# Four-layer sliding/full attention: pieces of four in one layer only, two key projections a chunk later, two weight slices in exponential buffers

## The chip, the cores and the metric

The kernel runs on one core of one Trainium2 chip. The metric is the device time of one execution in microseconds (us). TensorE does the matrix products, ScalarE (ACT) the exponentials, VectorE (DVE) and GpSimd (POOL) the elementwise work, and SyncE (SP) issues all DMAs in one order. "The clock" is TensorE's granted clock as a share of full speed.

## The reference

Four layers on x of shape [1, 2048, 512], 32 heads of 16. Layers 0 and 2 use weights A and a causal window of 256 tokens; layers 1 and 3 use weights B and attend to all tokens. Each layer adds its attention to x.

```python
def _A_ref(x, wqkv, wo):          # _B_ref is the same without the mask
    qkv = (x @ wqkv).reshape(B, S, 3, H, Dh).transpose(2, 0, 3, 1, 4)
    q, k, v = qkv[0], qkv[1], qkv[2]
    scores = jnp.einsum("bhqd,bhkd->bhqk", q, k) * (Dh ** -0.5)
    mask = (idx[:, None] - idx[None, :] >= 0) & (idx[:, None] - idx[None, :] < W)   # W = 256
    p = _softmax(jnp.where(mask[None, None], scores, -1e9), axis=-1)
    o = jnp.einsum("bhqk,bhkd->bhqd", p, v)
    return o.transpose(0, 2, 1, 3).reshape(B, S, D) @ wo

x = A_x
x = x + _A_ref(_layernorm(x), A_wqkv, A_wo)
x = x + _B_ref(_layernorm(x), B_wqkv, B_wo)
x = x + _A_ref(_layernorm(x), A_wqkv, A_wo)
x = x + _B_ref(_layernorm(x), B_wqkv, B_wo)
```

## The kernel before

**Attention.** The 2048 tokens are cut into four chunks of 512 queries. `attention(l, works)` goes through the chunks, and in each through eight groups of four heads (quads). A quad takes three steps in a sliding layer (24 steps a chunk) and sixteen in a full one. A step issues scores (line 722, TensorE) and two exponentials (line 726, ScalarE) into buffers with the tag `e`, of which there are six. In a sliding layer GpSimd then masks the edges of the window in place (lines 789 and 792). The product with the values (line 799 sliding, line 766 full) is issued two steps later. After that comes a share of *side work*.

**Side work.** All projections (queries, keys, values, output), the normalisations and the transposes of the neighbouring chunks and of the next layer are written as generators, wrapped in `Work` objects, and issued between the steps. Their matmuls have line 437, twelve to a group in one accumulation bank. The names are used below: `K(l, c)`, `Q(l, c)` and `VV(l, c)` are the keys, queries and values of chunk c of layer l, 48 matmuls each where all is done at once; `K3(c, ht)` and `Q3(c, ht)` are a quarter of those for layer 3 (12 matmuls, one group of 128 features `ht`); `OO(l, c)` is the output projection with the residual, after which the chunk's normalisation follows; `T(l, c)` transposes the normalised chunk by DMA (SyncE, line 497) into the `xc` tiles that the projections of layer l read; `NN` and `PR` are layer 0's normalisations and the preparation of weights; `F` fills buffers.

**Which side work belongs to which chunk** is written by hand: `side0(c)` and `side2(c)` for the chunks of layers 0 and 2, `tails[l]` and `lasts[l]` for what follows a sliding layer's last chunk. Whatever of a chunk's list is left over at its end is forced out there (`sd.finish()`), waiting where it has to.

**The planner.** TensorE's order is fixed as written. A small clock in the program adds 0.222 us for each matmul, and a `Work` is taken only when its dependencies are due by that clock. In each step of a sliding chunk, side work is issued up to the part of the list's cost that is due. `PH["run"]` says how many matmuls of a group are issued at once. It is set for each chunk: four if the list's cost is below seven matmuls a step, twelve otherwise. That gives four in chunk 0 of layer 0 and in all chunks of layer 2, and twelve in chunks 1 to 3 of layer 0.

```python
                if win:
                    PH["run"] = RUN if sd.cost < FEW * MM * sd.steps else 12
```

The order on the other engines and on SyncE's queue is worked out by the framework's scheduler from the program's order and priorities. SyncE's queue runs in order: an issue that waits for its source or its destination keeps back all behind it.

**Weights.** `weights(ty, s, n, ...)` loads a projection's weights from the DRAM tile `wd` into one of two buffers with the tag `w` (lines 398 and 400). A quarter of a projection takes a slice of 128 columns, 256 KB. A `Work` marked to use weights is opened, its load issued, only if the user of the buffer two places back is done; the planner then waits 8 us before its first matmul. `all_of(works, following)` issues a list of work to its end and may open the weights of the first of the following works.

**The tail of layer 2** is the list `tails[2]`, behind its last chunk, and then `lasts[2]`: K3(2,0), the output projection of the last chunk with its normalisation, four parts of the values, Q3(0,0), T(3,3) and K3(3,0), until layer 3's first scores can start.

Of the kernel before, what the change touches and what calls it, by code (L numbers as in the profile page):

```python
# [9 lines left out]
F32 = mybir.dt.float32  # L10
BF16 = mybir.dt.bfloat16
F16 = mybir.dt.float16
# [7 lines left out]
P = 128  # L20
NT = S // P
NC = D // P
HT = P // DH
NHT = H // HT
QC = 512
# [6 lines left out]
MM = 0.222  # L32
HEAD_START = 100
EB, XB, XNB, WB, VB, OB = 6, 4, 4, 2, 3, 5
RUN, FEW = 4, 7
L_MIN = 2.0 ** -90
L_SUM = 2.0 ** 60

# [149 lines left out]
def fast_path(ctx, tc, flag, a_x, a_wqkv, a_wo, b_wqkv, b_wo, out):  # L188
# [29 lines left out]
    def wait(us):  # L218

        return "wait", clock[0] + us  # L220
# [170 lines left out]

    def weights(ty, s, n, f0=0, f1=D):

        if (ty, s) in WT:
            return WT.pop((ty, s))
        w = wp.tile([P, NC, 2, D], F16, name=f"w{n}", tag="w", bufs=WB)
        if f1 - f0 == D:
            nc.sync.dma_start(w, wd[ty, s])
        else:
            nc.sync.dma_start(w[:, :, :, :f1 - f0], wd[ty, s][:, :, :, f0:f1])  # L400
        return w
# [103 lines left out]
    def project(l, s, c, act, ht=None, first=None):  # L505


        ty, n = l % 2, f"{l}_{s}_{c}" + ("" if ht is None else f"_h{ht}")
        if not first:
            w = weights(ty, s, n, *((0, D) if ht is None else (ht * P, (ht + 1) * P)))  # L510
            yield wait(8)
            xc = XC[l, c]
        if s == 0:
            dst = rows(qs[ty, c])
        elif ty == 0:
            dst = rows(kw[c])
        else:
            dst = rows(kf)[:, :, c * QC:(c + 1) * QC]
        sqs = {}
        for t in range(NHT) if ht is None else (ht,):  # L520
            ps = bank()
            w0 = t * P if ht is None else 0
            if first:
                yield from mms(ps, [(first[0][:, k, t * P:(t + 1) * P], first[1][:, k, :]) for k in range(NC)])
            else:
                yield from mms(ps, [(w[:, k, a, w0:w0 + P], xc[:, b, k, :]) for k in range(NC) for a, b in TERMS], 2.2)
            settle(not sqs)
            sp = vp.tile([P, 2, QC], F16, name=f"sp{n}_{t}", tag="sp", bufs=3)
            e = first[2][:, t:t + 1] if first else es[:, ty, s, t:t + 1]
            with tc.high_priority(HEAD_START):  # L530
                if act:
                    nc.scalar.activation(sp[:, 0], ps, AF.Copy, scale=e)  # L532
                else:
                    nc.vector.tensor_scalar(sp[:, 0], ps, e, None, op0=ALU.mult)  # L534
                nc.vector.scalar_tensor_tensor(sp[:, 1], ps, e, sp[:, 0], op0=ALU.mult, op1=ALU.subtract)  # L535
            sq = vp.tile([P, QC], BF16, name=f"sq{n}_{t}", tag="sq", bufs=NHT)
            if act:
                nc.scalar.activation(sq, sp[:, 0], AF.Square)
            else:
                nc.gpsimd.tensor_tensor(sq, sp[:, 0], sp[:, 0], ALU.mult)  # L540
            sqs[t] = sq

            d = dst[8 * t:8 * t + 8].rearrange("h (d b) n -> (h d) b n", b=4)
            if s:
                nc.sync.dma_start(d[:, 0:2], sp[:, 0:1].broadcast_to([P, 2, QC]))
                nc.sync.dma_start(d[:, 2], sp[:, 1])
            else:
                nc.sync.dma_start(d[:, 0:2], sp)
                nc.sync.dma_start(d[:, 2], sp[:, 0])
            yield -MM if PH["full"] else -PH["run"] * MM  # L550
        return sqs
# [409 lines left out]
    def later(f, *a):  # L961

        yield from f(*a)
# [4 lines left out]
    def attention(l, works):  # L968

        win = l % 2 == 0  # L970
        phase(l)
        load = load_win if win else load_full
        sd = None
        for t in range(NHT if l == 3 else 1):
            for c in range(NQ):
                qds = range(2 * t, 2 * t + 2) if l == 3 else range(NQD)
                if l == 1:

                    sd = sd or Side(NT * NQD // 2, works[0], works[1], 0.33)
                    while ("Q", 1, c) not in DONE:  # L980
                        sd.one(True)
                    settle()
                else:
                    sd = Side((3 if win else NT) * len(qds), works[t * NQ + c], works[t * NQ + c + 1], 0.34 if l == 3 and t < 2 else 0.0)
                if win:
                    PH["run"] = RUN if sd.cost < FEW * MM * sd.steps else 12
                ops = load(l, c, qds[0])
                for qd in qds:
                    if (l, c, qd) == (1, 0, NQD // 2):
                        sd.finish()  # L990
                        sd = Side(NT * NQD * NQ - NT * NQD // 2, works[1], works[2], 0.33)
                    nxt = load(l, c, qd + 1) if qd + 1 in qds else None
                    a = acc[qd % 2 if win else 0]
                    began = clock[0]
                    for f in (attn_win if win else attn_full)(l, c, qd, *ops, a):
                        clock[0] = max(clock[0], began + (2.4 if win else 1.8))
                        began = clock[0]
                        pvq.append([f])
                        flush(2)
                        sd.step()  # L1000
                        if win and not (PH["unit"] and PH["extra"]):
                            settle(False, 1 if PH["unit"] else 9)
                    pvq[-1].append(lambda l=l, c=c, qd=qd, a=a: epilogue(l, c, qd, a))
                    ops = nxt
                if l != 1 or c == NQ - 1:
                    sd.finish()
                if not win:
                    settle()
        flush(0)
        phase(None)  # L1010

    def T(l, c):
        return Work(later(lambda: transpose(l, c, XN.pop((l, c), ()))), 0.0, ("T", l, c), [("N", l, c)], aside=True)

    def K(l, c, act=True):
        return Work(later(keys, l, c, act), PK, ("K", l, c), [("T", l, c), ("P", l % 2, 1), ("P", l % 2, 0)], True)

    def Q(l, c, act=True, after=()):
        k = [("K", l, i) for i in (c - 1, c) if i >= 0] if l % 2 == 0 else list(after)
        return Work(later(queries, l, c, act), PK, ("Q", l, c), [("T", l, c), ("P", l % 2, 0)] + k, True)  # L1020

    def K3(c, ht, act=False):
        return Work(later(keys, 3, c, act, ht), PK / 4, ("K3", c, ht), [("T", 3, c)], True)

    def Q3(c, ht, act=False, after=()):
        return Work(later(queries, 3, c, act, ht), PK / 4, ("Q3", c, ht), [("T", 3, c), *after], True)

    def shifted(l, ht):
        key_shift(l, ht)
# [8 lines left out]
    def VV(l, c, act=True, halves=(0, 1), after=(), tiles=range(4)):  # L1038
        return Work(later(values, l, c, act, None, halves, tiles), PV * len(halves) * len(tiles) / 8, ("V", l, c, halves, tiles[0]),
                    [("T", l, c), ("P", l % 2, 2), *after], True)  # L1040

    def OO(l, c, tail=False):
        return Work(later(wo, l, c, tail), PO, ("N", l + 1, c), [("O", l, c, NHT - 1), ("P", l % 2, 3)], True)
# [14 lines left out]
    def all_of(works, following=()):  # L1058
        Side(1, works, following).finish()
# [65 lines left out]

    def side2(c):
        if c == 0:
            return [OO(1, 3), Q(2, 2), T(2, 3), K(2, 3)]
        if c == 1:
            return [OO(2, 0), Q(2, 3), T(3, 0), K3(0, 0, True)]  # L1130
        if c == 2:
            return [OO(2, 1), VV(2, 3), T(3, 1), K3(1, 0, True)]
        return [OO(2, 2), VV(3, 0, True, (0,)), T(3, 2)]

    def upper(l, c, tiles=range(4)):

# [8 lines left out]
    def side3(t, c):  # L1145
# [7 lines left out]
        if t < 2 and (t or c > 1):  # L1153
# [4 lines left out]
             [side3(t, c) for t in range(NHT) for c in range(NQ)]]  # L1158
    late = lambda l: [("N", l, 3)]
    tails = {0: [VV(1, 2, True, (0,)), OO(0, 3, True), VV(1, 1, True, (0,), late(1)), Q(1, 1, True, late(1)), T(1, 3), K(1, 3)],  # L1160
             2: [K3(2, 0, True), OO(2, 3, True), VV(3, 1, True, (0,), late(3)), VV(3, 2, True, (0,), late(3)), Q3(0, 0, True, late(3)), T(3, 3), K3(3, 0, True)]}
    lasts = {0: [VV(1, 3)], 2: [VV(3, 3, True, (0,)), VV(3, 0, True, (1,))]}
    for l in range(4):
        if l % 2 == 0:
            attention(l, works[l] + [tails[l]])
            all_of(tails[l], lasts[l])
            shift = Work(later(lambda: shifted(l + 1, 0 if l else None)), 0.0)
            shift.ready = clock[0] + 1.2
            all_of([shift] + lasts[l], works[l + 1][0])
        else:  # L1170
            attention(l, works[l] + [works[2][0] if l == 1 else [O3(3, 3)]])
    all_of([O3(3, 3)])
# [39 lines left out]
```

## Time and profile before

| | |
|---|---|
| median of 3 runs | 2757.3 us (2754.7 to 2758.5) |
| profiled execution | 2757.01 us, of which the span is 2755.3 us |
| clock, mean over the span | 0.99 |
| TensorE busy | 2636.7 us, 96% |
| ScalarE busy | 2380.4 us, 86% |
| VectorE, GpSimd busy | 957.1 us, 571.2 us |

Where the layers lie in the span, from the first exponential of each chunk:

| us from the start | what |
|---|---|
| 66 to 143, 143 to 246, 246 to 361, 361 to 456 | layer 0, chunks 0 to 3 |
| 456 to 513 | tail of layer 0 |
| 513 to 1463 | layer 1 (full) |
| 1466 to 1539, 1539 to 1609, 1609 to 1674, 1674 to 1737 | layer 2, chunks 0 to 3 |
| 1737 to 1785 | tail of layer 2 |
| 1786 to 2737 | layer 3 (full) |

How to read the lines below. In the table of stretches, each row has the stretch, its length, the busy time and the instructions of each engine, the clock, the mean share of the DMA engines in use and what they moved. In the waits, a row has the engine, the tile and line that waited, what it waited for, and then the microseconds in total, the times and the longest. In a timeline, a row has start, length, engine, line, operation, tiles and shapes, and in brackets the idle time ahead of it and what ended it. "PE" is TensorE; "SPq" is a DMA issue on SyncE.

### The profile page before, as it was taken

How to read it: one execution, taken by the hardware profiler on the slowest of the kernel's cores; microseconds unless marked ns; L12 is line 12 of the kernel's file. 1: busy time of each engine (PE TensorE's matmuls, PEld its weight loads, DVE VectorE, ACT ScalarE, POOL GpSimd, SP SyncE). 2: the span in 40 equal slices, each digit the busy share in tenths (PEclk: the TensorE clock that was granted, in tenths of full speed). 3: DMA queues.
4: the chain of work that ended last, by engine and by line, in shares of the span. 5: the costliest groups of instructions: out<-in, count | busy, mean ns of one | idle time of the engine just before them, and what ended most of it. 6: DMA issues, size and time to landing. Idle time of an engine off the chain costs nothing.

```text
span 2755.3 us, 59647 instructions
## 1 busy us (share of the span) xinstructions
PE 2636.7 (96%) x24358; PEld 773.8 (28%) x24358; DVE 957.1 (35%) x2059; ACT 2380.4 (86%) x2687; POOL 571.2 (21%) x1129
## 2 busy tenths in 40 slices
PE   8988999999999999999999999899999999999997
PEld 4333344322222222222222333522222222222221
DVE  7677756111221113211315577512222222222222
ACT  3665565799999999999997678399999999999997
POOL 2576663000100000000005678100000000000000
PEclk9999999999999999999999999999999999999999
DMA  6876776521323223222324565723333343333331
GB/s 218 229 220 197 215 225 175 166 78 57 108 83 84 87 86 100 89 67 77 114 68 148 156 183 161 185 62 104 111 112 122 120 123 102 102 110 114 98 95 56
DMA packets 318269, 344.78 MB, mean 125 GB/s; under 512 B 114080, under 2 KB 234144, under 8 KB 311968
## 3 DMA queue, kind: packets, MB, share of 16 engines
q1 hardware_dynamic: 317984, 340.86, 41.2%
q8 instruction: 193, 3.16, 0.5%
q14 instruction: 92, 0.75, 0.1%
HBM read 228.07 MB, written 96.99 MB: 118 GB/s over the span
## 4 chain that ended last, share of the span: by engine, by line
PE 76%; DVE 8%; ACT 7%; issue 5%; DMA 3%; POOL 1%; SPq 0%; ACTq 0%; DVEq 0%; POOLq 0%
PE acc L766 30%; PE s L722 20%; PE b L437 10%; PE acc L434 10%; ACT e L726 7%; PE acc L799 4%; PE bs L437 2%; DVE ot L694 1%; DVE xh L476 1%; DVE sp L535 1%; DVE xh L470 1%; DVE xn L470 1%; DMA x<-in_A_x_dram 0%; DMA kt<-kf 0%; DMA kt<-kw 0%
## 5 line engine op out<-in xcount | busy, mean ns | idle before, releaser
L726 ACT ACTIVATE e<-s 128x1024 f32<-128x1024 f32 (+2 forms) x2432 | 2245.4, 1118 | 113.0 <-PE s L722 102.2
L766 PE MATMUL acc<-e,vt 128*17 128x512 f32 x8192 | 1078.5, 598 | 5.6 <-DVE ot L694 4.7
L722 PE MATMUL s<-qt,kt 64*128 64x512 f16 (+3 forms) x5504 | 773.2, 355 | 53.3 <-ACT e L726 28.4
L722 PEld LDWEIGHTS <-kt 64*128 64x128 f16 x5504 | 199.9, 94 | 798.4 <-issue 769.0
L792 POOL TENSOR_SCALAR_AFFINE_SELECT e<-e 128x256 f32<-128x256 f32 x512 | 230.0, 456 | 123.2 <-ACT e L726 122.1
L766 PEld LDWEIGHTS acc<-e,vt 128*17 128x17 f32 x8192 | 136.2, 95 | 383.4 <-issue 350.8
L694 DVE STREAM_TRANSPOSE ot<-acc 128x512 f32<-128x512 f32 x128 | 91.5, 715 | 411.2 <-PE acc L766 317.5
L710 POOL TENSOR_TENSOR oh<-o,oh 128x512 f16<-128x512 f32 x31 | 36.0, 1161 | 883.0 <-DVE oh L709 883.0
L789 POOL TENSOR_SCALAR_AFFINE_SELECT e<-e 128x256 f32<-128x256 f32 x448 | 201.7, 456 | 71.7 <-ACT e L726 69.3
L799 PE MATMUL acc<-e,vt 128*17 128x384 f32 (+2 forms) x2816 | 198.9, 393 | 4.4 <-POOL e L789 2.5
L437 PE MATMUL b<-xc,w 128*128 128x512 f16 x672 | 166.2, 395 | 16.5 <-DMA qs<-m_None 6.4
L540 POOL TENSOR_TENSOR sq_h<-sp_h 128x512 bf16<-128x512 f16 x27 | 28.1, 1041 | 480.9 <-DVE sp_h L534 480.9
L534 DVE TENSOR_SCALAR sp<-acc,es 128x512 f16<-128x512 f32 x28 | 20.9, 748 | 288.9 <-PE acc L434 277.1
L534 DVE TENSOR_SCALAR sp_h<-acc,es 128x512 f16<-128x512 f32 x27 | 20.3, 751 | 290.1 <-PE acc L434 290.1
L540 POOL TENSOR_TENSOR sq<-sp 128x512 bf16<-128x512 f16 x28 | 29.1, 1041 | 397.1 <-DVE sp L534 397.1
L434 PE MATMUL acc<-xc,w_h 128*32 128x512 f16 x1296 | 108.9, 380 | 2.3 <-DVE km L573 2.3
L434 PE MATMUL acc<-xc,w 128*32 128x512 f16 x1344 | 108.9, 379 | 0.3
L646 DVE COPY vt<-acc 128x256 f32<-128x256 f32 (+1 forms) x36 | 18.5, 513 | 256.4 <-PE acc L434 256.4
L532 ACT ACTIVATE sp<-b,es 128x512 f16<-128x512 f32 x56 | 38.5, 687 | 79.9 <-PE b L437 76.7
L681 DVE TENSOR_TENSOR dx<-acc,gcol 128x512 f32<-128x512 f32 x60 | 41.5, 692 | 176.6 <-PE acc L434 176.6
L437 PEld LDWEIGHTS <-w 128*128 128x128 f16 x720 | 67.5, 100 | 121.3 <-issue 50.4
L434 PE MATMUL acc<-wo,oh 128*32 128x512 f16 x1296 | 101.3, 379 | 0.0
(170 smaller groups left out, 1813.3 us busy)
## 6 DMA issues: line engine op xcount, KB each, us to landing
kt<-kf SPq DMA_DIRECT2D x128, 512.0 KB
qt<-qs SPq DMA_DIRECT2D x128, 256.0 KB
xd<-x SPq DMA_DIRECT2D x96, 256.0 KB
x<-xd SPq DMA_DIRECT2D x96, 256.0 KB
w<-wd SPq DMA_DIRECT2D x20, 1024.0 KB
kt<-kw SPq DMA_DIRECT2D x64, 256.0 KB
qs<-sp SPq DMA_DIRECT2D x48, 256.0 KB
wo<-wd SPq DMA_DIRECT2D x12, 1024.0 KB
```

What stands on the lines that cost most here:

```text
L434: nc.tensor.matmul(ps[g:g + 32], a[:, g:g + 32], b, start=(i == 0), stop=(i == len(pairs) - 1), skip_group_check=True)
L437: nc.tensor.matmul(ps, a, b, start=(i == 0), stop=(i == len(pairs) - 1))
L470: norm1 = lambda o: nc.vector.tensor_scalar(o, xs[i], mv[:, i, 0:1], y[:, i:i + 1], op0=ALU.subtract, op1=ALU.mult)
L540: nc.gpsimd.tensor_tensor(sq, sp[:, 0], sp[:, 0], ALU.mult)
L681: nc.vector.tensor_tensor(d, ps, gcol[1], ALU.mult)
L694: nc.vector.transpose(ot.rearrange("p b r -> p (b r)"), a)
L722: nc.tensor.matmul(ps[:, h, s0:s0 + wd_], kt[R * h:R * h + R, pr, kc:kc + P], qt[R * h:R * h + R, pr, qc:qc + wd_], start=True, stop=True)
L726: nc.scalar.activation(e[:, :, w0:w1], ps[:, :, w0:w1], AF.Exp, scale=SCALE)
L766: nc.tensor.matmul(a[32 * h:32 * h + DH + 1, :], V[l, qd // 4, j // 8][:, j % 8, 4 * (qd % 4) + h, :], es_[h // 2][:, h % 2, :], start=(j ...
L789: nc.gpsimd.affine_select(v, v, pattern=[[0, 2], [-1, P]], compare_op=ALU.is_gt, fill=0.0, base=0, channel_multiplier=1)
L792: nc.gpsimd.affine_select(v, v, pattern=[[0, 2], [1, P]], compare_op=ALU.is_ge, fill=0.0, base=0, channel_multiplier=-1)
L799: nc.tensor.matmul(a[32 * h:32 * h + DH + 1, q * P:(q + nb) * P], V[l, (4 * c + j) // 4][:, j % 4, 4 * qd + h, :], es_[h // 2][:, h % 2, s ...
```

## The change

Three things change. First, `PH["run"]` is four in every chunk of layer 2 and twelve in every chunk of layer 0: only chunk 0 of layer 0 differs by that.

Second, in layer 2 three key projections are placed later: K(2,3) from the end of chunk 0's list to the head of chunk 1's; K3(0,0) from the end of chunk 1's list to chunk 2's, ahead of T(3,1); K3(1,0) from the end of chunk 2's list to chunk 3's, ahead of VV(3,0).

Third, behind layer 2's last chunk a new function `ahead` takes two of the six exponential buffers and loads the weight slices of Q3(0,0) and K3(3,0) into them. These two works no longer take a `w` buffer, and the planner no longer waits 8 us for their weights. `all_of` for the last values of a sliding layer no longer opens the next layer's first weights. In the order that results, Q3(0,0) stands ahead of VV(3,2) in the tail, where it stood behind it before.

```diff
-RUN, FEW = 4, 7
+RUN = 4
...
     def weights(ty, s, n, f0=0, f1=D):
-        if (ty, s) in WT:
-            return WT.pop((ty, s))
+        for k in ((ty, s), n):
+            if k in WT:
+                return WT.pop(k)
...
         if not first:
+            here = n in WT
             w = weights(ty, s, n, *((0, D) if ht is None else (ht * P, (ht + 1) * P)))
-            yield wait(8)
+            yield wait(0 if here else 8)
...
-                    PH["run"] = RUN if sd.cost < FEW * MM * sd.steps else 12
+                    PH["run"] = RUN if l else 12
...
-    def K3(c, ht, act=False):
-        return Work(later(keys, 3, c, act, ht), PK / 4, ("K3", c, ht), [("T", 3, c)], True)
-
-    def Q3(c, ht, act=False, after=()):
-        return Work(later(queries, 3, c, act, ht), PK / 4, ("Q3", c, ht), [("T", 3, c), *after], True)
+    def K3(c, ht, act=False, own=False):
+        return Work(later(keys, 3, c, act, ht), PK / 4, ("K3", c, ht), [("T", 3, c)], not own)
+
+    def Q3(c, ht, act=False, after=(), own=False):
+        return Work(later(queries, 3, c, act, ht), PK / 4, ("Q3", c, ht), [("T", 3, c), *after], not own)
+
+    def ahead(ty, s, n, ht):
+        e = pp.tile([P, 2, QC], F32, name=f"we{n}", tag="e", bufs=EB)
+        WT[n] = e.rearrange("p a n -> p (a n)").bitcast(F16)[:, :NC * 2 * P].rearrange("p (k a f) -> p k a f", k=NC, a=2)
+        nc.sync.dma_start(WT[n], wd[ty, s][:, :, :, ht * P:(ht + 1) * P])
...
     def side2(c):
         if c == 0:
-            return [OO(1, 3), Q(2, 2), T(2, 3), K(2, 3)]
+            return [OO(1, 3), Q(2, 2), T(2, 3)]
         if c == 1:
-            return [OO(2, 0), Q(2, 3), T(3, 0), K3(0, 0, True)]
+            return [K(2, 3), OO(2, 0), Q(2, 3), T(3, 0)]
         if c == 2:
-            return [OO(2, 1), VV(2, 3), T(3, 1), K3(1, 0, True)]
-        return [OO(2, 2), VV(3, 0, True, (0,)), T(3, 2)]
+            return [OO(2, 1), VV(2, 3), K3(0, 0, True), T(3, 1)]
+        return [OO(2, 2), K3(1, 0, True), VV(3, 0, True, (0,)), T(3, 2)]
...
-             2: [..., Q3(0, 0, True, late(3)), T(3, 3), K3(3, 0, True)]}
+             2: [..., Q3(0, 0, True, late(3), True), T(3, 3), K3(3, 0, True, True)]}
...
             attention(l, works[l] + [tails[l]])
+            if l:
+                ahead(1, 0, "3_0_0_h0", 0)
+                ahead(1, 1, "3_1_3_h0", 0)
             all_of(tails[l], lasts[l])
...
-            all_of([shift] + lasts[l], works[l + 1][0])
+            all_of([shift] + lasts[l])
```

More of the change, by code (lines that the diff above doesn't have):

```diff
@@ L1160, in fast_path @@
     tails = {0: [VV(1, 2, True, (0,)), OO(0, 3, True), VV(1, 1, True, (0,), late(1)), Q(1, 1, True, late(1)), T(1, 3), K(1, 3)],
-             2: [K3(2, 0, True), OO(2, 3, True), VV(3, 1, True, (0,), late(3)), VV(3, 2, True, (0,), late(3)), Q3(0, 0, True, late(3)), T(3, 3), K3(3, 0, True)]}
+             2: [K3(2, 0, True), OO(2, 3, True), VV(3, 1, True, (0,), late(3)), VV(3, 2, True, (0,), late(3)), Q3(0, 0, True, late(3), True), T(3, 3), K3(3, 0, True, True)]}
     lasts = {0: [VV(1, 3)], 2: [VV(3, 3, True, (0,)), VV(3, 0, True, (1,))]}
```

## The prediction

> **What bounds the kernel now.** I read the page first, then busy time in stretches cut at the chunk borders, then TensorE's waits, then the timelines around the longest of them.
>
> ```profile
> span 2755.3 us, 59647 instructions
> PE 2636.7 (96%) x24358; PEld 773.8 (28%) x24358; DVE 957.1 (35%) x2059; ACT 2380.4 (86%) x2687; POOL 571.2 (21%) x1129
> ```
>
> ```profile
> core 0: us, PE busy (x) PEld busy (x) DVE busy (x) ACT busy (x) POOL busy (x), PEclk, DMA share, GB/s
> 65.00:143.00 78.00, 69.03 (x525) 23.44 (x525) 48.65 (x110) 49.00 (x72) 43.90 (x96) 0.93 0.86 225
> 143.00:246.00 103.00, 88.68 (x788) 36.10 (x784) 71.65 (x148) 62.73 (x79) 71.89 (x149) 0.97 0.73 227
> 246.00:361.00 115.00, 103.51 (x846) 41.65 (x844) 87.07 (x158) 68.80 (x90) 75.73 (x140) 0.94 0.70 206
> ...
> 1466.00:1539.00 73.00, 64.88 (x516) 22.36 (x513) 45.85 (x107) 44.57 (x63) 41.28 (x96) 0.95 0.62 181
> 1539.00:1600.00 61.00, 58.95 (x642) 22.38 (x641) 43.29 (x99) 49.30 (x56) 50.75 (x120) 1.00 0.55 163
> 1600.00:1609.00 9.00, 5.97 (x40) 2.27 (x41) 4.90 (x10) 2.37 (x4) 4.96 (x12) 0.82 1.08 297
> 1609.00:1674.00 65.00, 63.27 (x688) 24.65 (x684) 43.96 (x103) 49.26 (x56) 53.00 (x125) 1.00 0.60 175
> 1674.00:1737.00 63.00, 59.44 (x701) 24.84 (x700) 46.70 (x101) 48.56 (x54) 56.94 (x133) 0.97 0.52 137
> 1737.00:1785.00 48.00, 41.05 (x281) 26.87 (x279) 24.05 (x54) 12.68 (x26) 0.00 (x0) 1.00 0.72 204
> ```
>
> ```profile
> 513.00:1463.00 950.00, 938.97 (x9207) 223.10 (x9203) 183.66 (x425) 946.19 (x1024) 47.56 (x46) 1.00 0.27 83
> ```
>
> The stretches are: layer 0's chunks 0 to 2; layer 2's chunk 0, chunk 1 with its last 9 us apart, chunk 2, chunk 3, and the tail behind it. The last row is layer 1: ScalarE is busy 946.19 of 950 us with exponentials. Layers 1 and 3 are paced there, and no moved matmul shortens them. In the sliding layers TensorE is the bound: what a stretch can lose is its idle time and its slow clock. In layer 2's chunk 0 that is 73 - 64.88 = 8.1 us and a clock of 0.95; its neighbours idle 2.1, 3.0, 1.7 and 3.6. TensorE's waits in 1466 to 1785 name them:
>
> ```profile
> PE s L722 <- ACT e L726: 6.7, 13, 1.0
> PE b L437 <- DMA qs<-m_None: 6.4, 1, 6.4
> PE b L437 <- DMA w_h<-wd: 3.7, 2, 2.6
> PE b L437 <- DVE op L704: 2.8, 1, 2.8
> PE acc L799 <- DVE ot L694: 1.9, 1, 1.9
> ```
>
> The 6.4 and the 2.8 are single holes, in front of K(2,3) and of K3(0,0), the two key projections that the change puts a chunk later. The 3.7 are the tail's two weight slices. TensorE's timeline (start, us) has the places:
>
> ```profile
> 1506.37 0.28 PE L722 MATMUL s<-qt,kt 64*128 64x256 f16 x2 [0.45 <-ACT e L726]
> 1507.59 0.28 PE L722 MATMUL s<-qt,kt 64*128 64x256 f16 x2 [0.93 <-ACT e L726]
> ...
> 1518.81 5.26 PE L437 MATMUL b<-xc,w 128*128 128x512 f16 x12 [6.42 <-DMA qs<-m_None]
> ...
> 1543.05 1.04 PE L437 MATMUL b<-xc,w 128*128 128x512 f16 x4
> 1544.02 0.61 PE L722 MATMUL s<-qt,kt 64*128 64x384 f16 x8
> 1544.56 1.06 PE L799 MATMUL acc<-e,vt 128*17 128x128 f32 x16
> 1545.55 1.04 PE L437 MATMUL b<-xc,w 128*128 128x512 f16 x4
> ...
> 1604.53 4.03 PE L437 MATMUL b<-xc,w_h 128*128 128x512 f16 x12 [2.80 <-DVE op L704]
> ...
> 1762.00 2.76 PE L437 MATMUL b<-xc,w_h 128*128 128x512 f16 x12 [1.13 <-DMA w_h<-wd]
> 1767.67 2.76 PE L437 MATMUL b<-xc,w_h 128*128 128x512 f16 x12 [2.59 <-DMA w_h<-wd]
> ```
>
> From 1543.05 to 1545.55 is one step with one piece of four side matmuls: 2.50 us without a gap, so such steps are as dense as TensorE gets. The group at 1518.81 took 5.26 us against 2.76 for the same twelve matmuls at 1762.00: it came out of the hole at the slow clock. The hole's releaser is named after a store; what the group reads is xc of chunk 3, whose last transpose was issued on SyncE 7.5 us earlier:
>
> ```profile
> 1511.30 1.91 SPq L497 DMA_TRANSPOSE xc<-xh  x1
> ```
>
> **Part 1, keys a chunk later (layer 2).** No matmul is added or removed, they change places, so dense time goes with them at 0.25 us each and cancels; holes do not move with them.
> - K(2,3) leaves chunk 0. The hole goes (6.42) and the slow group (5.26 - 2.76 = 2.50): -8.9. Chunk 0 then holds 24 pieces for 24 steps, so steps that ran empty while the planner saved pieces get one: the two exponential waits 0.45 and 0.93 go, -1.4. In chunk 1, K(2,3) can't start before the fourth step or so, some 8 us after the transposes; that covers it barely. Without that cover the hole is back (rival 1).
> - K3(0,0) leaves the end of chunk 1, where it was forced out against OO's last operands: 2.80 and 4.03 - 2.76 = 1.27 go, -4.1. In chunk 2 it stands behind VV(2,3), with inputs a chunk old. K3(1,0) becomes 12 matmuls more in chunk 3, between OO(2,2) and VV(3,0); dense, nothing.
> - The new wait: T(2,3) and T(3,0), the transposes, are now the last side work of chunks 0 and 1, and SyncE issues in order. The next chunk's query and key loads are queued behind them, and the scores wait for those loads. A transpose holds the queue 1.9 us (row above), three of them 4.5 (row 1758.92 below). Bounds: 0 if normalisation is done a quad before the border, 6 if the last three transposes stand between, over two borders. I take 3, near the one-transpose row for each. A gain is excluded, since the loads only move back.
> - Chunk 3's wait for ot (1.9) sits behind a normalisation that stays: 0.
>
> Layer 2: -8.9 - 1.4 - 4.1 + 3.0 = -11.4, bounds -14.4 to -8.4, and beyond by rival 1.
>
> [...] The trace has a 2.80 us hole followed by a slow group (4.03 against 2.76). [...] The trace is followed.
>
> **Part 2, the tail's weights in exponential buffers.**
>
> ```profile
> 1735.11 0.33 SPq L398 DMA_DIRECT2D wo<-wd  x1
> ...
> 1739.87 2.75 PE L437 MATMUL b<-wo,oh 128*128 128x512 f16 x12
> ...
> 1758.92 4.52 SPq L497 DMA_TRANSPOSE xc<-xh  x3
> 1764.16 0.54 SPq L400 DMA_DIRECT2D w_h<-wd  x1
> 1766.49 0.41 SPq L548 DMA_DIRECT2D qs<-sp_h  x1
> ```
>
> The slices of Q3(0,0) and K3(3,0) no longer wait for one of the two weight buffers: -1.13, and of the 2.59 about 2.4, since the transposes that K3(3,0) also reads end their issue at 1763.44 and the rest is theirs: -3.5. Against this: the two preloads (256 KB each) stand on SyncE directly ahead of wo for layer 2's last chunk. That load is issued at 1735.11 and its first matmul starts at 1739.87, with nothing to spare. At the tail's 204 GB/s the two take 2.5 us; their buffers come free about a microsecond ahead of the old issue of wo, so I charge 1.4 (bounds 0 to 7.0, rival 3). And Q3(0,0) now runs before the last transposes, whose issue comes behind its stores: two at 0.41 and as much for their producer, +1.6 (bounds 0 to 3). Tail: -3.5 + 1.4 + 1.6 = -0.5, bounds -3.5 to +6.5.
>
> The weights for layers 1 and 3 are no longer opened early by the last tail work. Layer 1 idles on TensorE for 950 - 938.97 = 11 us, spread over 512 steps, so late side work fits: 0, or 1 us if their first steps press on ScalarE.
>
> **Part 3, pieces of twelve in layer 0's chunk 0.** The old rule gave four there; the new one gives twelve to all of layer 0.
>
> ```profile
> 115.39 0.82 PE L722 MATMUL s<-qt,kt 64*128 64x384 f16 x4 [4.64 <-DMA kt<-kw]
> 116.14 1.05 PE L799 MATMUL acc<-e,vt 128*17 128x256 f32 x8
> 117.13 3.59 PE L437 MATMUL b<-w,xc 128*128 128x512 f16 x8
> ...
> 122.13 1.90 PE L437 MATMUL b<-w,xc 128*128 128x512 f16 x8
> ```
>
> Its 144 side matmuls make 12 groups for 24 steps, so about 12 steps have none and wait for the exponentials: 1.38 us over the two empty steps above, 0.69 each, 8.3 in all. The wait of 4.64 for a key load and the slow group behind it (3.59 - 1.90 = 1.7) hang on the order of stores and loads in the chunk; with groups finished whole their stores leave earlier, and I let them go. Busy 69.0 - 1.7 = 67.3, with 8.3 idle 75.6, against 78: -2.4. Bounds: -11 if the preparation of the next weights, which VectorE and GpSimd do and which moves forward with the groups, also eases chunks 1 and 2 (idle 14.3 and 11.5 there); +8.3 if no wait goes; more is rival 2.
>
> **Sum.** The profiled execution took 2757.0 us (1.7 around its span), the median is 2757.3, so it stands for the runs. 2757.0 - 11.4 - 0.5 - 2.4 = 2742.7.
>
> **Rivals.**
> 1. The hole goes along with K(2,3): chunk 1 reaches it before the transposes have landed. For it: 7.5 us passed from issue to use. Against: about four steps of 2.0 to 2.5 us lie between. If half the hole stays (4.5) and the loads cost 6 instead of 3: 2750.
> 2. Slower: layer 0 with twelve. The empty steps cost 8.3, and GpSimd's and ScalarE's weight preparation, issued earlier, stands ahead of the masks and exponentials of chunk 0 as it does in chunk 1, which idles 14.3. No wait goes: 2742.7 + 2.4 + 8.3 + 14.3 = 2768. It decides once layer 0 loses over 17.4 us (2762.5 less 2745.1). Against it: chunk 0 idles only 9 us with the same preparations in it.
> 3. wo comes late. A 256 KB slice took 3.5 us from its issue at 1764.16 to its group at 1767.67; two in a row ahead of wo are 7.0 instead of 1.4: 2748. [...]
> 4. More: the loosened preparation helps chunks 1 and 2 too, layer 0 gains its bound of 11 instead of 2.4: 2734.
> 5. It doesn't do what it says: the planner forces the moved keys out at the ends of chunks 2 and 3 as it did before, and the queue eats the rest: 2757.
>
> **How the numbers follow.** Forecast 0.45 (2735 to 2749); rival 1 0.17; rival 2 0.14; rival 3 0.05; rival 4 0.13; rival 5 0.06. About 0.2%, 5.5 us, is what a measurement of this kernel can tell from nothing. Faster by over that: forecast, 3, 4 and two thirds of 1, 0.74. Within it: 5 and the rest of 1, 0.12. Slower: 0.14. The range 2730 to 2759 leaves out rival 2 and the far ends of rivals 4 and 5.
>
> **What would show it.** Right: in layer 2's chunk 0 no wait over 2 us at L437 and the chunk near 54 us, chunk 1 near 72; no forced group at the end of chunk 1; Q3(0,0) and K3(3,0) without a wait for w_h; layer 1's rows as they are. Wrong: a wait at L437 early in chunk 1 (rival 1); a wait of over 2 us for qt or kt at the starts of chunks 1 and 2; a wait at the group of wo behind 1735 (rival 3); layer 0's first chunk over 80 us or chunks 1 and 2 longer than 103 and 115 (rival 2).

## The result and the profile after

The changed kernel takes 2750.75 us (median of 7 runs, 2746.72 to 2753.32) against 2759.27 for the kernel before on the same chips (7 runs). The ratio is 0.9969, 95% interval 0.9957 to 0.9981: 8.5 us faster. The forecast was 14. The total lies in the range, but the profile shows that its terms do not stand as they were forecast. Lines of the changed kernel are one or two higher than before (437 is 438, 722 is 724).

Busy time by stretch, cut at the chunk borders of the profile after (span 2749.2 us). First layer 0's chunks 0 to 2, then layer 2's chunks 0 to 3 and its tail:

```profile
core 0: us, PE busy (x) PEld busy (x) DVE busy (x) ACT busy (x) POOL busy (x), PEclk, DMA share, GB/s
64.00:146.00 82.00, 70.11 (x527) 24.74 (x528) 53.42 (x115) 50.30 (x75) 47.03 (x99) 0.96 0.84 231
146.00:241.00 95.00, 85.44 (x784) 35.18 (x782) 76.99 (x158) 61.78 (x78) 70.64 (x139) 1.00 0.82 244
241.00:347.00 106.00, 98.97 (x844) 40.36 (x844) 77.65 (x145) 66.30 (x85) 72.27 (x150) 0.98 0.70 212
...
1456.00:1511.00 55.00, 51.67 (x462) 17.10 (x460) 42.96 (x102) 40.40 (x56) 42.32 (x97) 1.00 0.57 171
1511.00:1591.00 80.00, 73.51 (x718) 28.42 (x717) 43.03 (x103) 55.19 (x64) 51.51 (x125) 0.96 0.57 178
1591.00:1666.00 75.00, 67.23 (x688) 25.25 (x688) 49.63 (x113) 49.49 (x55) 56.58 (x132) 0.93 0.67 171
1666.00:1728.00 62.00, 57.86 (x678) 24.34 (x678) 46.74 (x103) 48.66 (x54) 54.68 (x128) 1.00 0.53 150
1728.00:1778.00 50.00, 43.66 (x321) 28.40 (x321) 23.84 (x54) 13.46 (x28) 1.64 (x5) 1.00 0.68 201
```

Layer 0 has gained. Its chunk 0 is 4 us longer than the 78 of before (idle 11.9 in place of 9.0), but chunks 1 and 2 take 95 and 106 us in place of 103 and 115, with most of the slow clock gone (1.00 and 0.98 in place of 0.97 and 0.94). Layer 1 starts at 500 us in place of 513. Layer 2 has lost: chunk 0 takes 55 us in place of 73, as forecast, but chunk 1 takes 80 in place of 70 (61 and 9) and chunk 2 takes 75 in place of 65, together 272 in place of 271 at these cuts. Not all of chunk 1's 10 us is loss: it holds 144 side matmuls in place of 108 (K(2,3) came in, K3(0,0) went out), and 36 matmuls at 2.76 us for twelve are 8 us. Chunk 2 holds 108 as before, so its 10 us are loss. Counted between the first and the last exponential of the layer it is 272.2 in place of 268.4, 3.8 us more.

TensorE's waits from layer 2's start to its tail's end say where:

```profile
PE s L724 <- ACT e L728: 8.4, 14, 1.9
PE b L438 <- DMA wv<-wd: 5.3, 1, 5.3
PE s L724 <- DMA qt<-qs: 4.8, 2, 4.1
PE b L438 <- DMA xc<-xh: 3.6, 1, 3.6
PE b L438 <- DMA wo<-wd: 2.4, 1, 2.4
```

The two old holes (6.4 in front of K(2,3), 2.8 in front of K3(0,0)) are gone. In their place TensorE waits for query loads (4.1) and for a weight load (5.3). The two tail waits for w_h (3.7) became waits for wo and xc (6.0). Their places in TensorE's timeline, and SyncE's around the first two:

```profile
1521.49 0.61 PE L724 MATMUL s<-qt,kt 64*128 64x128 f16 x8 [4.08 <-DMA qt<-qs]
1522.03 1.47 PE L801 MATMUL acc<-e,vt 128*17 128x256 f32 x16
1523.44 3.13 PE L438 MATMUL b<-xc,w 128*128 128x512 f16 x8
...
1603.00 1.89 PE L438 MATMUL b<-wv,xc 128*128 128x512 f16 x4 [5.30 <-DMA wv<-wd]
...
1735.56 2.75 PE L438 MATMUL b<-wo,oh 128*128 128x512 f16 x12 [2.40 <-DMA wo<-wd]
1763.15 2.75 PE L438 MATMUL b<-xc,we_h 128*128 128x512 f16 x12 [3.57 <-DMA xc<-xh]
```

```profile
1511.03 0.41 SPq L399 DMA_DIRECT2D w<-wd  x1
...
1513.05 0.47 SPq L754 DMA_DIRECT2D qt<-qs  x1
...
1594.48 0.38 SPq L399 DMA_DIRECT2D wv<-wd  x1
1595.03 0.39 SPq L550 DMA_DIRECT2D qs<-sp  x1
1595.47 4.10 SPq L498 DMA_TRANSPOSE xc<-xh  x1
1599.66 0.54 SPq L754 DMA_DIRECT2D qt<-qs  x1
```

At the start of chunk 1 a whole projection's weights (1 MB) go out at 1511.03, two microseconds ahead of the query load at 1513.05; TensorE gets on at 1521.49. At the start of chunk 2 the weights for VV(2,3) go out at 1594.48 and are used 8.5 us later. Behind the hole the matmuls are slow: eight take 3.13 us at 1523.44, four take 1.89 at 1603.00, where 1.90 and 1.04 are usual; the granted clock over these two rows is 0.60 and 0.50.

### The profile page after: what moved, and what is told of

The parts are those of the page before. It is cut to its first block, busy times and chain, and to the rows that moved or that the text cites. A ratio compares the mean times of both kernels' runs of the same rounds, so it can differ in the third digit from the quotient of the medians.

```text
span 2749.2 us, 59656 instructions
## 1 busy us (share of the span) xinstructions
PE 2632.0 (96%) x24358; PEld 772.6 (28%) x24358; DVE 955.6 (35%) x2059; ACT 2380.7 (87%) x2687; POOL 570.4 (21%) x1129
## 4 chain that ended last, share of the span: by engine, by line
PE 74%; DVE 8%; ACT 7%; issue 4%; DMA 3%; POOL 2%; SPq 1%; ACTq 0%; DVEq 0%; POOLq 0%
PE acc L768 31%; PE s L724 19%; PE acc L435 10%; PE b L438 9%; ACT e L728 7%; PE acc L801 4%; PE bs L438 1%; DVE ot L696 1%; DVE sp L537 1%; POOL wr L345 1%; DVE xh L477 1%; DMA qt<-qs 1%; DVE xn L471 1%; DVE xh L471 1%; POOL e L791 0%
## 5 line engine op out<-in xcount | busy, mean ns | idle before, releaser
L438 PE MATMUL b<-xc,w 128*128 128x512 f16 x672 | 159.6, 385 | 11.9 <-DVE sp L537 7.8
```

The source lines that it names most:

```text
L438: nc.tensor.matmul(ps, a, b, start=(i == 0), stop=(i == len(pairs) - 1))
```

## The experiments

**Each part alone.** Four kernels on one chip: three have one part of the change each on top of the kernel before, the fourth is the changed kernel without part 1.

```diff
 pieces_only:  the kernel before with
-                    PH["run"] = RUN if sd.cost < FEW * MM * sd.steps else 12
+                    PH["run"] = RUN if l else 12
 keys_only:    the kernel before with the new side2
 tail_only:    the kernel before with weights, K3, Q3, ahead, tails and all_of of the change
 keys_back:    the changed kernel with the old side2
```

> The kernel before with part 3 alone: twelve matmuls to a piece in all of layer 0, four in all of layer 2. Theory A (the profiles after: layer 1 starts 12.3 us earlier and everything ahead of it differs by the pieces alone): 12 us faster than before, some 2747, and a little more if layer 1's 2 us loss belongs to the weights that are no longer opened early. Rival B (the forecast's own size for layer 0): 2.4 us faster, 2757. Rival C (the gain needs the other parts): no change.

> The kernel before with part 1 alone: K(2,3), K3(0,0) and K3(1,0) a chunk later. Theory A (the profile after: layer 2's four chunks take 3.9 us more): 4 us slower than before, 2763. Rival B (the forecast): 11.4 us faster, 2748. Rival D: the holes after are owed to when layer 2 starts, and with the old start they fall otherwise: anywhere between, with chunk 1 and 2 not near 80 and 75 us.

> The kernel before with part 2 alone: the two weight slices in exponential buffers, no early opening of weights behind a sliding layer. Theory A (the profile after: the tail of layer 2 1.0 us shorter, layer 1's first chunk 2.0 us longer): 1 us slower, 2760, not to be told from before. Rival B (the forecast): 0.5 us faster. Rival E (the slices hold back the load of wo): 5 us slower.

> The changed kernel with part 1 undone: the three key projections where they were before. Theory A (the parts add up): the 3.9 us that layer 2 lost come back, 2747, 12 us faster than before. Rival B (part 1 is what gains): slower than the changed kernel by up to 11 us, about 2760.

| kernel | median us | ratio to before, 95% interval |
|---|---|---|
| pieces_only | 2745.11 | 0.9950, 0.9936 to 0.9963 |
| keys_only | 2764.57 | 1.0015, 1.0006 to 1.0024 |
| tail_only | 2758.89 | 1.0006, 0.9996 to 1.0015 |
| keys_back | 2747.89 | 0.9955, 0.9941 to 0.9969 |

At 2758.4 us for the kernel before, the ratios of the first three are -13.8, +4.1 and +1.7 us, in sum -8.0; the changed kernel has -8.5. The parts add up, theory A holds for all four, and the forecast's own sizes for layer 0 and layer 2 (rivals B) fall. In keys_only chunks 1 and 2 take 80 and 75 us, as in the changed kernel, so rival D falls too. The pieces in one chunk of layer 0 bring all of the gain; the keys take 4 us of it away; the tail is nothing that these runs can tell from zero. pieces_only alone is the faster kernel by the medians (2745 against 2751); by the ratios it is 0.9950 against 0.9969, and the intervals touch.

A profile is of one execution, so the lengths of the chunks are worth checking over all of them. Counted from the first exponential of each chunk, the three profiles with pieces of four in layer 0's chunk 0 and the scaling where it was (before, keys_only, tail_only) have 76.9 to 79.8 us in chunk 0, 102.7 to 105.9 in chunk 1 and 113.2 to 114.9 in chunk 2. The eight profiles with pieces of twelve and the scaling where it was have 80.2 to 82.3, 94.5 to 96.6 and 105.3 to 107.1. Layer 2's chunk 2 takes 65.3 or 65.4 us in the seven profiles with the keys in their old places, and 74.6 to 75.4 in the three with the keys moved and no load held back (the changed kernel, keys_only and due18, which comes below).

The tail alone, in its timeline: the waits for w_h are replaced by longer ones.

```profile
1749.08 2.75 PE L438 MATMUL b<-wo,oh 128*128 128x512 f16 x12 [3.54 <-DMA wo<-wd]
...
1776.73 4.08 PE L438 MATMUL b<-xc,we_h 128*128 128x512 f16 x12 [3.64 <-DMA xc<-xh]
```

**Why layer 0 gained.** In the kernel before, ScalarE's timeline around the longest wait of chunk 2, and GpSimd's beside it:

```profile
255.53 0.63 ACT L346 ACTIVATE w<-wr 128x512 f16<-128x512 f32 x1 [4.42 <-POOL wr L345]
256.07 0.67 ACT L532 ACTIVATE sp<-b,es 128x512 f16<-128x512 f32 x1
256.64 1.01 ACT L726 ACTIVATE e<-s 128x1024 f32<-128x1024 f32 x1
```

```profile
253.66 0.44 POOL L789 TENSOR_SCALAR_AFFINE_SELECT e<-e 128x256 f32<-128x256 f32 x1
254.07 1.43 POOL L345 TENSOR_TENSOR wr<-wr,wd 128x512 f32<-128x512 f32 x1
```

A cast of the weight preparation (line 346) stands on ScalarE and waits 4.42 us for GpSimd's scaling (line 345), which waits its turn behind six masks (250.41 to 254.07). The exponential of the next scores stands behind that cast, so TensorE waits too:

```profile
257.70 0.61 PE L722 MATMUL s<-qt,kt 64*128 64x384 f16 x4 [3.63 <-ACT e L726]
```

The group of ScalarE's casts, from 60 to 460 us, shows it as a sum: before, after and with the pieces alone (the last column is idle time ahead of them, by releaser).

```profile
L346 ACT ACTIVATE w<-wr 128x512 f16<-128x512 f32 x24 | 15.1, 633 | 22.6 <-POOL wr L345 17.5 <-DVE wr L345 4.9
```

```profile
L346 ACT ACTIVATE w<-wr 128x512 f16<-128x512 f32 x25 | 15.1, 634 | 12.8 <-POOL wr L345 8.5 <-DVE wr L345 4.3
```

```profile
L346 ACT ACTIVATE w<-wr 128x512 f16<-128x512 f32 x25 | 15.1, 634 | 12.7 <-POOL wr L345 8.5 <-DVE wr L345 4.2
```

TensorE's waits for exponentials in chunks 1 and 2, first before (143 to 246, 246 to 361), then after (146 to 243, 243 to 347):

```profile
PE s L722 <- ACT e L726: 8.2, 8, 2.9
PE s L722 <- ACT e L726: 6.0, 6, 3.6
```

```profile
PE s L724 <- ACT e L728: 4.4, 7, 1.2
PE s L724 <- ACT e L728: 0.4, 2, 0.2
```

The two longest, 2.9 and 3.6, are gone. The pieces of twelve do not touch the preparation's own work; they move when it falls. Before, GpSimd's batch of scalings at the border runs from 144.6 to 151.7 us, in chunk 1, and the first cast behind it starts at 145.9. In the changed kernel the batch runs from 135.5 to 144.2 and is through before chunk 1 (146), and two of its casts start in chunk 0, at 139.6. So the next experiment left the pieces alone and moved the scaling off GpSimd:

```diff
-        mul = lambda k: (nc.vector if act else nc.gpsimd).tensor_tensor(raw[:, k, :], raw[:, k, :], dnb, ALU.mult)
+        mul = lambda k: nc.vector.tensor_tensor(raw[:, k, :], raw[:, k, :], dnb, ALU.mult)
```

> The kernel before (pieces of four in layer 0's chunk 0), with the scaling of the raw weights in the preparation moved from GpSimd to VectorE; the rest as before. Theory H (layer 0 gained with pieces of twelve because the exponentials of chunks 1 and 2 no longer stand on ScalarE behind a cast that waits 2.8 and 4.4 us for GpSimd's scaling, itself behind the masks): these waits go here too, chunks 1 and 2 at 95 and 107 us in place of 100 and 113, 8 to 12 us faster, 2748. Rival I (the gain is in the pieces' own order, stores earlier): no gain, and up to 10 us slower, since VectorE takes 16 scalings more.

> The same edit on the kernel with the pieces alone (2745). Theory H: the waits are gone already, so it gains no more than 3 us or nothing: 2742 to 2746, and the two gains don't add. Rival I: the edit does here what it did on the kernel before, so the difference of the two kernels stays 13 us.

scale_dve: 2741.92 us, ratio 0.9943 (0.9930 to 0.9956). pieces_scale_dve: 2739.89, ratio 0.9934 (0.9921 to 0.9946). With the old pieces the edit brings 15.7 us; on top of the new pieces it brings 4 by the ratios, within their intervals. Two gains of 13.8 and 15.7 make 18.2 together, not 29.5: they are largely the same one. Theory H holds in the main, rival I falls. In scale_dve no wait of TensorE for exponentials in layer 0 is over 1.7 us, and chunk 2 takes 105.3 us in place of 114.9. Chunk 1 takes 99.9 in place of 102.7, less of a gain than was expected: TensorE waits 2.3 and 2.0 us for VectorE there at line 557, where one wait of 1.3 stood before. ScalarE's casts wait for VectorE only, and no longer for masks:

```profile
L346 ACT ACTIVATE w<-wr 128x512 f16<-128x512 f32 x24 | 14.9, 645 | 14.3 <-DVE wr L345 14.3
```

One thing is not separated: the edit also takes all 20 of these scalings off GpSimd (POOL in chunk 1 falls from 71.9 to 65.2 us), which may help the masks by itself.

**Why layer 2 lost.** First theory: two weight loads at the borders. Both were to be mended at once, on top of pieces_only:

```diff
+                    (self.name != ("Q", 2, 3) or any(x.name == ("K", 2, 3) and x.begun for x in wused)) and   # in may_open
...
-            yield wait(8)
+            yield wait(18 if (l, c) == (2, 3) else 8)      # in values
```

> The kernel with the pieces alone (2745), with part 1 as in the change, and two mends to when weights are asked for: the weights of Q(2,3) are not loaded before K(2,3) has begun, and VV(2,3) is due 18 us after its load was opened in place of 8, so that OO(2,1) goes first in chunk 2. Theory F (what part 1 lost is two 1 MB weight loads at chunk borders: one ahead of qt and kt in SyncE's queue at the start of chunk 1, 4.1 us and the slow clock after it, some 6; one that VV waits for in chunk 2, 5.3 us and 4 of slow clock): chunk 1 near 74 us and chunk 2 near 66 in place of 80 and 75, in all 2745 + 4 - 15 = 2734. Rival G (a border without ready side work costs that much whichever load is first, so other waits take their place): chunks stay near 80 and 75, 2745 to 2749.

> As keys_mended, but only K(2,3) is late; K3(0,0) and K3(1,0) stand at the ends of chunks 1 and 2 as before. Theory F: chunk 0 at 54 us, chunk 1 with the K3(0,0) group at its end at 77, chunk 2 near 66: 2738, a few us behind keys_mended by the forced group. If the forced K3(0,0) also gives the next weight load its time, as rival G would have it: as fast as keys_mended or faster.

keys_mended: 2742.34 us, ratio 0.9950 (0.9936 to 0.9964); k23_mended: 2742.06, ratio 0.9949 (0.9936 to 0.9961). No better than the pieces alone by the ratio, and 8 us short of the 2734 that was expected. The stretches of chunks 1 and 2 of keys_mended, and SyncE's and TensorE's rows at the first border:

```profile
1508.00:1588.00 80.00, 73.59 (x728) 28.71 (x727) 48.45 (x113) 55.81 (x64) 53.75 (x129) 0.96 0.67 200
1588.00:1654.00 66.00, 62.95 (x692) 24.61 (x690) 42.85 (x102) 49.57 (x55) 54.18 (x129) 1.00 0.60 177
```

```profile
1508.52 0.38 SPq L398 DMA_DIRECT2D wo<-wd  x1
...
1509.98 0.38 SPq L752 DMA_DIRECT2D qt<-qs  x1
```

```profile
1518.17 0.61 PE L722 MATMUL s<-qt,kt 64*128 64x128 f16 x8 [4.00 <-DMA kt<-kw]
```

Chunk 2 is mended (66), chunk 1 is not (80): with Q(2,3)'s weights held back, the weights of OO(2,0) took their place in the queue, 1.5 us ahead of the query load. k23_mended is level with keys_mended, but it differs in two things: both K3 stand where they were, and VV(2,3) has its old due time of 8 us. The two together are worth nothing here; each by itself is not shown. Its chunks 1 and 2:

```profile
1510.00:1592.00 82.00, 76.66 (x748) 30.03 (x752) 48.21 (x113) 56.40 (x66) 53.26 (x128) 0.96 0.68 190
1592.00:1657.00 65.00, 62.19 (x675) 24.18 (x666) 43.63 (x103) 49.42 (x56) 53.79 (x127) 1.00 0.62 187
```

So chunk 2 is mended without the due time of 18 too.

Two more kernels followed from this. due18 puts the due time alone into the changed kernel. keys_mended2 holds back OO(2,0)'s load as well, by a one-column copy from K(2,3)'s first result into the buffer that the load fills:

```diff
+        if n == "o2_0":                                                    # in weights
+            nc.vector.tensor_copy(w[:, 0, 0, 0:1], LATE[0][:, 0, 0:1])
...
+            if (l, s, c) == (2, 1, 3) and not LATE:                        # in project
+                LATE.append(sp)
...
+                    (self.name not in (("Q", 2, 3), ("N", 3, 0)) or LATE) and   # in may_open, for the line above
```

> The changed kernel with one constant changed: VV(2,3) is due 18 us after its weights' load was opened in place of 8, so OO(2,1) goes first in layer 2's chunk 2. Theory F (the wait of 5.3 us for these weights and the slow clock behind it are what chunk 2 lost): chunk 2 at 66 us in place of 75, the whole 9 us faster than the changed kernel, 2742. Rival G (OO(2,1) then waits for its own operands as long): no change, 2751.

> The kernel with the pieces alone, as before, for a comparison on one chip: 2745, 13 us faster than before.

> As keys_mended, but now no 1 MB load at all goes out at the border of chunks 0 and 1: the weights of OO(2,0) are loaded only behind K(2,3)'s first group (a one-column copy on VectorE from that group's result into the buffer holds the load back), so qt and kt of quads 1 and 2 go ahead of them in SyncE's queue. In keys_mended the weights of OO(2,0) had only taken the place of those of Q(2,3). Theory F: the waits of 4.0 and 1.9 us for kt and qt at the start of chunk 1 and the slow clock behind them go, chunk 1 at 73 us in place of 79, 6 us faster than keys_mended, 2736. Rival G (the loads wait for something else, the stores of Q(2,2) or the transposes): chunk 1 stays near 79, 2742.

> keys_mended2 with the scaling of the raw weights on VectorE as in pieces_scale_dve. If the gains of the two layers add (pieces_scale_dve was 2 us ahead of the pieces alone): 2 us faster than keys_mended2, 2734, and with that ahead of all others. If not: no difference from keys_mended2.

| kernel | median us | ratio to before, 95% interval |
|---|---|---|
| due18 | 2751.70 | 0.9970, 0.9958 to 0.9981 |
| pieces_again | 2746.33 | 0.9949, 0.9935 to 0.9962 |
| keys_mended2 | 2736.17 | 0.9924, 0.9911 to 0.9938 |
| all_mended | 2730.42 | 0.9897, 0.9881 to 0.9912 |

Lines of keys_mended2 are two to four higher than before.

due18 was a miss: the changed kernel's time is unmoved. Its timeline in chunk 2 shows why:

```profile
1605.87 1.04 PE L724 MATMUL s<-qt,kt 64*128 64x128 f16 x8 [8.01 <-DMA qt<-qs]
```

```profile
1594.55 0.38 SPq L399 DMA_DIRECT2D wv<-wd  x1
1595.19 0.32 SPq L550 DMA_DIRECT2D qs<-sp  x1
1595.56 3.54 SPq L498 DMA_TRANSPOSE xc<-xh  x1
1599.20 0.71 SPq L754 DMA_DIRECT2D qt<-qs  x1
```

Without the wait for wv, TensorE waits 8.01 us for the query load that stands in the queue behind it, behind the 1 MB load and the last transpose of T(3,0). The named wait had only covered a second one, so the wait named in the profile after was not the cause by itself. Whether the load's place in the queue or the late transpose costs more is not separated. keys_mended speaks for the transpose: there the weights for VV(2,3) also go out ahead of a query load (1584.24 and 1587.62), with T(3,0) through by 1578.7, and the waits for qt around this border are 1.95 and 1.33 us. In keys_mended2 these transposes are through well ahead of the border at 1584, and the query loads of chunk 1 go out 14 us ahead of OO(2,0)'s weights:

```profile
1510.34 0.45 SPq L756 DMA_DIRECT2D qt<-qs  x1
...
1524.87 0.38 SPq L400 DMA_DIRECT2D wo<-wd  x1
...
1572.86 2.76 SPq L499 DMA_TRANSPOSE xc<-xh  x2
```

```profile
1509.00:1584.00 75.00, 72.41 (x724) 28.53 (x725) 48.86 (x115) 55.54 (x64) 53.13 (x128) 0.98 0.72 215
1584.00:1649.00 65.00, 63.05 (x688) 24.64 (x688) 43.12 (x102) 49.20 (x55) 54.20 (x129) 1.00 0.61 176
```

Chunk 1 takes 75 us and chunk 2 65, and the kernel is 10 us faster than the pieces alone on the same chip by the medians (2736.17 against 2746.33); by the ratios it is 7 us, and the intervals just overlap. What mended chunk 2 was most likely the order: with Q(2,3) held back, OO(2,0) and its normalisation go first and T(3,0) with them. k23_mended, which holds Q(2,3) back and has no due time of 18, bears this out: its last transpose of T(3,0) is issued by 1581.0, 10 us ahead of the border, and chunk 2 takes 65 us. But there K3(0,0) also stands between T(3,0) and the border, and no run has the hold alone, so the order is argued and not shown by itself.

all_mended adds the scaling on VectorE: 2730.42, 28 us faster than before and the fastest of all. Against keys_mended2 that is 5.8 us by the medians, where 2 were expected (7 by the ratios, whose intervals touch): the scaling's gain comes on top of layer 2's.

## Why the prediction was right in its total, and where its steps failed

- **Part 1, the holes.** Right in place for chunk 0: the hole and the slow group went, and the chunk takes 55 us. The named 54 does not follow from the terms, though: 48 matmuls at 0.25 us leave the chunk as well, so 73 - 12 - 8.9 - 1.4 is 50.7. In the same way chunk 1 comes to 76 (70 + 9 - 4.1 + 1.5) and not to 72. What fell short in chunk 0 are the waits for exponentials: 1.4 was to go, and they rose from 1.7 to 3.2 us. For K3(0,0) -4.1 was booked; with the pieces alone its forced group comes behind a hole of 2.3 us and at full clock (1.00 in chunks 1 and 2), and k23_mended, where it stands at the end of chunk 1 too, is 0.3 us from keys_mended. So no run shows the 4.1 as a gain.
- **Part 1, the new wait.** The step that failed. The loads behind the transposes were named and priced at 3 us over two borders (bounds 0 to 6). In the changed kernel the first border costs a wait of 4.08 and slow groups behind it (0.4 and 1.2 us over the usual in the two rows shown); the second costs some 10 us in waits and slow clock (5.30 at the weights, and 0.93 over the chunk), with the matmuls of the chunk as many as before. The step had counted the time that transposes hold SyncE's issue (1.9 each), and not the 1 MB weight loads, which by the planner's rule go out at the border, because a weight buffer comes free there. At the first border holding them back took 5 us off the chunk (80 in keys_mended, 75 in keys_mended2); at the second, load and transpose are not separated. Part 1 was forecast as -11.4 and is +4.1 (interval 1.7 to 6.6). With the loads held back, and the due time of 18, the kernel is 7 to 10 us faster than the pieces alone: moving the keys pays, and the wait at the borders is the term that was mis-sized.
- **Rival 1** did not happen: the first group of K(2,3), at 1523.44, waited for no transpose. The loss came through the scores.
- **Part 2, the tail.** Near: -0.5 forecast, +1.7 with an interval from -1.1 to +4.1 measured. Both exchanges were as named and larger than charged: wo comes late (2.40 and 3.54 us where 1.4 had been charged, inside the bounds of 0 to 7 and short of rival 3), and the transposes are later (xc 3.57 where 1.6 had been charged). Layer 1, for which 0 or 1 us had been allowed, took 952.7 us from its first to its last exponential in the profile after and 950.7 before, but 951.3 and 951.4 in tail_only and keys_back, which have the same tail, so the 2 us are not tied to the weights.
- **Part 3, pieces of twelve.** Forecast -2.4, measured -13.8 (interval 10.2 to 17.7). Chunk 0 itself went the other way: 4 us longer where 2.4 less had been worked out, idle 11.9 us and busy 70.1 where 8.3 and 67.3 had been named; the wait for kt stayed with 2.2 us. The gain came in chunks 1 and 2 by the mechanism of rival 4, the preparation of weights, given 0.13 and a bound of 11. The step that failed counted empty steps in one chunk and took the preparation as a side effect, where it was the cause of the two longest waits for exponentials in the next two.
- **The slow group behind the 2.80 us hole.** Its 1.27 us were booked as the trace had them, and that was right: from 1.3 us into the group on the granted clock was 0.50 (last section), so the 1.27 us belonged to the clock.
- The total came out inside the range since two terms erred by 11 and by 15 us in opposite directions. That is luck and no support for either. Three of the named signs of being wrong appeared: the wait of 4.08 us for qt at the start of chunk 1, the wait of 2.40 at the group of wo, and layer 0's first chunk over 80 us.

## What to carry to other kernels

When side work is moved away from a hole, list what its absence brings forward on the DMA queue: a weight buffer that comes free at a chunk border sends a large load just ahead of the smaller loads that the next scores need (here 1 MB, 2.0 us ahead of the query load; with such loads held back the chunk took 75 us in place of 80). When work moves from one stretch to another, take it out before comparing their lengths: most of chunk 1's growth here was work, and all of chunk 2's was loss. A wait that the profile names can cover a second one (here 5.30 us for weights, and 8.01 for a query load when that wait was gone), so try the mend alone before calling it the cause. And where one engine does both the critical exponentials and preparation for later, a delay of the preparation's producer can reach the exponentials (here a cast waited 4.42 us on ScalarE, and TensorE 3.63 us for the exponential behind it): look for a wait on that engine in front of work that isn't urgent, and move its producer off the busy queue.

## What the runs showed of the hardware

Whether TensorE is slow after a hole did not follow the hole's length. A group of twelve took 4.03 us behind 2.80 us (before) and 4.08 behind 3.64 (tail_only), but 2.76 behind 2.59 (before) and 2.75 behind 3.57 (changed kernel). In the kernel before the granted clock was still 1.00 from 1602.42 to 1605.84 us, in which TensorE was busy for 1.31 of the 3.42 us, and 0.50 from 1605.84 to 1609.25: it fell 1.3 us after the hole had ended. What decides whether the clock falls behind a hole, no run here shows.
